# Cluster attention and two MoE layers on one core: the first pair's similarities from a dense centroid table, the last output tile in two halves, new order tables

## The chip, the cores and the metric

The kernel runs on one core of a Trainium2 chip. The metric is device time in microseconds (us) for one execution. A core has five engines that run side by side and wait for each other through semaphores: TensorE (PE; its weight loads are listed apart as PEld), VectorE (DVE), ScalarE (ACT), GpSimd (POOL) and SyncE (SP), which here only issues DMA transfers.

## The reference

Three stages, one after the other. `C` is 16 clusters, there are 2 batches of 8 heads with 768 positions of 64 values.

```python
q_n, k_n, c_n = (t / (norm(t) + 1e-6) for t in (q, k, centroids))
q_assign = argmax(einsum('bhsd,hcd->bhsc', q_n, c_n))
k_assign = argmax(einsum('bhsd,hcd->bhsc', k_n, c_n))
scores = where(q_assign[..., None] == k_assign[..., None, :], scale * q @ k.T, -1e9)
x = softmax(scores) @ v                      # then to [1536 tokens, 512]
h = x @ w_in; solu = h * softmax(h)
x = (layernorm(solu) * g_ln) @ w_out         # 512 -> 1024 -> 512
out = ((x @ w_a) * (x @ w_b)) @ w_out2       # 512 -> 1536 -> 512
```

## The kernel before

Heads are worked on in pairs: 8 pairs (batch, two heads), 96 score steps of 128 queries by 768 keys (`score`, L1014), each followed by the maximum (DVE L1018), the exponential (ACT L1022), transposes of the result (`turn`, L1046) and, for every three steps, the product with v (`apply`, L1070). Then come the first MoE layer (`moe_h` L1162, `moe_x2` L1254) and the second one (`quartet` L1384, `moe2_y` L1441), whose 12 output tiles are summed in PSUM, added to an accumulator in SBUF by DVE (L1457) and written out (SP L1460).

Every fp32 value that TensorE multiplies precisely is held as a high part and a low part ("hi" and "lo"). A head's operand `kq` has four slots of 768 columns; in slots 0 and 1 one half of the 128 rows holds the hi and the other half the lo part of q or k.

The mask is not applied to the scores one by one. Each query and key gets a one-hot row of its cluster, and these rows are a second matmul into the same PSUM tile. So before the first score of a pair can be complete, this must be done: transpose q and k (`direct`, PE L784, three transposes of 128 columns for each of q/k, head, half of the positions), take hi (ACT L791), a copy of hi into the other rows (ACT L796 for q, POOL L793 for k), take lo (DVE L797), multiply with the normalized centroids (`do_sim0`, PE L810), find the largest of the 16 (`do_arg`, DVE L879 to L890), transpose the one-hots (`do_oh0`, PE L905) and copy them into `kq` (ACT L916, DVE L914). This is the path of pair 0, and only of it: for the others `do_sims` (PE L841, L845) does it in other shapes, long ahead of need.

The centroids are normalized by seven small instructions (DVE L702 to L712, one POOL L704), doubled to 128 columns, transposed into PSUM (PE L717: rows 0 to 63 and 64 to 127 hold the same), and put into the table `cb`, which is mostly zeros: upper rows go to one set of columns and lower rows to another, hi (ACT L726) and lo (DVE L727). With this `cb`, one `do_sim0` matmul has 64 columns (hi and lo by row half by 16 clusters) and DVE has to add four of them up (L813).

To fill times in which TensorE has nothing to do at the start, `FILL` = 16 transposes of the identity (L719) and `WARM` = 8 matmuls of 512 columns (L732) stand in its queue; their results are not used.

The order of everything is written out: each engine's instructions are planned operations with a number, and the table `SEQ` lists for each engine the numbers in the order in which they are issued. Semaphores only make an engine wait; no engine ever passes a waiting instruction in its own list.

Of the kernel before, what the change touches and what calls it, by code (L numbers as in the profile page):

```python
# [49 lines left out]
        862, 829, 865, 853, 851, 873, 822, 866, 868, 887, 824, 876, 878, 900, 836, 890, 892, 903, 906, 904, 930,  # L50
        937, 935, 883, 947, 933, 944, 942, 910, 940, 954, 950, 948, 914, 973, 957, 959, 990, 979, 983, 961, 981,
        991, 997, 976, 993, 1004, 1015, 1006, 986, 1026, 1022, 1000, 1024, 1029, 1032, 1011, 1030, 1055, 1018,
        1041, 1044, 1046, 1020, 1074, 1058, 1036, 1069, 1060, 1038, 1075, 1081, 1077, 1051, 1084, 1096, 1086,
        1112, 1109, 1101, 1099, 1137, 1117, 1115, 1113, 1148, 1121, 1144, 1146, 1165, 1140, 1162, 1156, 1151,
        1154, 1176, 1168, 1166, 1158, 1190, 1181, 1172, 1204, 1179, 1201, 1199, 1186, 1197, 1216, 1211, 1193,
        1209, 1238, 1195, 1221, 1219, 1252, 1205, 1250, 1248, 1207, 1255, 1256, 1258, 1269, 1262, 1267, 1226,
        1287, 1265, 1282, 1285, 1280, 1278, 1310, 1290, 1288, 1292, 1317, 1313, 1315, 1327, 1320, 1322, 1324,
        1328, 1330, 1334, 1358, 1348, 1337, 1339, 1355, 1344, 1353, 1351, 1365, 1361, 1375, 1359, 1379, 1370,
        1368, 1386, 1384, 1382, 1389, 1392, 1390, 1403, 1396, 1399, 1401, 1413, 1408, 1406, 1410, 1416, 1414,
        1420, 1444, 1434, 1425, 1423, 1477, 1430, 1427, 1478, 1488, 1435, 1432, 1489, 1514, 1437, 1515, 1448,  # L60
        1454, 1547, 1544, 1541, 1548, 1580, 1577, 1581, 1613, 1574, 1610, 1614, 1646, 1607, 1643, 1647, 1670,
        1640, 1671, 1664, 1667, 1722, 1723, 1688, 1716, 1719, 1746, 1692, 1747, 1770, 1740, 1743, 1771, 1838,
        1689, 1693, 1696, 1700, 1697, 1701, 1764, 1839, 1793, 1832, 1767, 1788, 1794, 1789, 1835, 1803, 1798,
        1856, 1804, 1799, 1888, 1884, 1859, 1885, 1889, 1881, 1878, 1892, 1896, 1915, 1912, 1893, 1897, 1918,
        1922, 1923, 1919, 1930, 1926, 1931, 1927, 2053, 2055, 2057, 2059, 2061, 2064, 2066, 2068, 2070, 2072,
        2074, 2076, 2079, 2081, 2083, 2085, 2090, 2092, 2094, 2100, 2105, 2151, 2153, 2158, 2160, 2134, 2138,
        2133, 2137, 2135, 2168, 2162, 2201, 2173, 2205, 2203, 2209, 2207, 2141, 2136, 2143, 2147, 2149, 2139,
        2212, 2214, 2145, 2218, 2217, 2216, 2220, 2219, 2221, 2243, 2245, 2250, 2252, 2254, 2260, 2265, 2269,
        2229, 2231, 2230, 2273, 2271, 2277, 2275, 2312, 2232, 2234, 2233, 2309, 2307, 2282, 2280, 2308, 2310,
        2325, 2327, 2332, 2334, 2336, 2342, 2311, 2317, 2315, 2313, 2347, 2375, 2377, 2379, 2321, 2319, 2323,  # L70
        2391, 2381, 2383, 2386, 2388, 2418, 2420, 2425, 2390, 2392, 2394, 2395, 2427, 2429, 2435, 2440, 2409,
        2393, 2405, 2446, 2444, 2406, 2404, 2408, 2407, 2484, 2483, 2450, 2448, 2455, 2452, 2501, 2457, 2508,
        2503, 2487, 2512, 2510, 2485, 2486, 2491, 2489, 2488, 2518, 2523, 2551, 2553, 2555, 2557, 2559, 2562,
# [1463 lines left out]
```

## Time and profile before

| | |
|---|---|
| time, median of 3 runs | 681.65 us (680.88 to 681.95) |
| profiled execution | 681.25 us |
| its span in the trace | 679.4 us |
| PE / PEld busy | 671.3 us (99%) / 576.0 us (85%) |
| DVE / ACT / POOL busy | 523.1 / 389.4 / 285.8 us |
| chain that ended last | PE 93%, DVE 4%, ACT 1%, DMA 1%, issue 1% |

The span is the time from the first to the last event of the trace; the execution has 1.85 us around it. A busy share is the sum of the durations over the span. Matmuls overlap each other, so that a busy PE may still be one whose next matmul could have started earlier; how densely it works is seen from the starts of neighbouring instructions.

### The profile page before, as it was taken

The numbers are of one execution on the slowest core, as the hardware profiler recorded it, in microseconds if no ns is written. First come the engines' busy times: TensorE is split into PE (matmuls) and PEld (weight loads), VectorE is DVE, ScalarE is ACT, GpSimd is POOL, SyncE is SP. The second block draws the span as 40 slices with busy tenths as digits, with TensorE's granted clock in tenths as the row PEclk, the third lists the DMA queues.
The fourth block names the chain that finished last, engine by engine and source line by source line (L and its number), as shares of the span: only waits on it lengthen the run. The fifth ranks groups of instructions, "written<-read, shape, count | busy, mean of one in ns | idle before, by whom it ended". The sixth has DMA issues, their size and how long they took to land.

```text
span 679.4 us, 10935 instructions
## 1 busy us (share of the span) xinstructions
PE 671.3 (99%) x3910; PEld 576.0 (85%) x3910; DVE 523.1 (77%) x943; ACT 389.4 (57%) x820; POOL 285.8 (42%) x323
## 2 busy tenths in 40 slices
PE   8999999999999999999999999999999999999997
PEld 7777777777777767888999999998989999989996
DVE  6978797798778878999869359796876757977436
ACT  5877777768677864574464555554654543534221
POOL 4024554635456433244445477644335432542000
PEclk9999999999999999999999999999999999999999
DMA  4367447473722612110211002132112212110005
GB/s 140 97 157 192 115 119 189 121 169 83 203 85 71 161 38 63 32 62 32 66 59 62 1 1 91 65 116 72 62 63 94 93 63 63 63 62 32 1 0 187
DMA packets 33094, 58.49 MB, mean 86 GB/s; under 512 B 3848, under 2 KB 21904, under 8 KB 33040
## 3 DMA queue, kind: packets, MB, share of 16 engines
q1 hardware_dynamic: 33040, 57.79, 30.0%
q8 instruction: 31, 0.51, 0.3%
q14 instruction: 23, 0.19, 0.1%
HBM read 36.74 MB, written 3.15 MB: 59 GB/s over the span
## 4 chain that ended last, share of the span: by engine, by line
PE 93%; DVE 4%; ACT 1%; DMA 1%; issue 1%; SPq 0%; DVEq 0%; ACTq 0%
PE psT L1384 25%; PE psS L1162 10%; PE psO L1070 10%; PE psS L1441 9%; PE psS L1014 9%; PE psT L1046 9%; PE psO L1254 5%; PE psM L1254 5%; PE psO L1441 2%; PE psM L1441 2%; PE psT L1237 2%; PE psM L750 1%; PE psM L841 1%; PE psM L1099 1%; PE psM L845 1%; DMA R<-R 1%
## 5 line engine op out<-in xcount | busy, mean ns | idle before, releaser
L1384 PE MATMUL psT<-R 128*128 128x384 f32 x1008 | 181.8, 336 | 0.4 <-DVE F L1363 0.3
L1384 PEld LDWEIGHTS psT<-R 128*128 128x128 f32 x1008 | 175.8, 188 | 4.8 <-ACT F L1359 1.3
L483 POOL TENSOR_TENSOR R<-F,R 128x256 fp32r<-128x256 f32 (+3 forms) x92 | 109.7, 1202 | 98.0 <-ACT R L1294 51.5
L595 POOL TENSOR_TENSOR F<-F 128x512 int32<-128x512 int32 x45 | 60.8, 1350 | 110.3 <-DVE F L591 96.3
L1359 ACT COPY F<-psT 128x384 f32<-128x384 f32 x108 | 51.5, 480 | 91.9 <-PE psT L1384 84.8
L1022 ACT ACTIVATE F<-psS,mxn 128x768 f32<-128x768 f32 x96 | 86.7, 905 | 23.2 <-DVE mxn L1018 16.7
L1018 DVE TENSOR_REDUCE mxn<-psS 128x1 f32<-128x768 f32 x96 | 90.4, 951 | 10.6 <-PE psS L1014 9.4
L1014 PE MATMUL psS<-R 128*128 128x512 f32 (+3 forms) x384 | 89.9, 358 | 0.9 <-DMA R<-R 0.6
L1046 PE MATMUL psT<-ident,F 128*128 128x128 f32 x576 | 85.8, 275 | 0.2
L1046 PEld LDWEIGHTS psT<-ident,F 128*128 128x128 f32 x576 | 65.4, 140 | 13.3 <-ACT F L1022 6.3
L1014 PEld LDWEIGHTS psS<-R 128*128 128x128 f32 (+1 forms) x384 | 65.6, 190 | 12.2 <-ACT F L1022 2.6
L1441 PE MATMUL psS<-R 128*128 128x512 f32 x288 | 74.9, 391 | 0.0
L1162 PE MATMUL psS<-R 128*128 128x512 f32 x288 | 69.3, 394 | 0.0
L1070 PE MATMUL psO<-F 128*64 128x384 f32 x384 | 69.0, 494 | 0.0
L1053 DVE COPY F<-psT 128x384 f32<-128x384 f32 x96 | 52.8, 550 | 15.5 <-PE psT L1046 14.2
L1441 PEld LDWEIGHTS psS<-R 128*128 128x128 f32 x288 | 53.8, 188 | 10.3
L1162 PEld LDWEIGHTS psS<-R 128*128 128x128 f32 x288 | 53.0, 188 | 10.5
L485 DVE TENSOR_TENSOR R<-F,R 128x384 fp32r<-128x384 f32 (+1 forms) x72 | 53.3, 753 | 8.5 <-ACT R L1373 3.9
L1363 DVE TENSOR_TENSOR F<-psT,F 128x384 f32<-128x384 f32 x48 | 26.7, 555 | 39.8 <-PE psT L1384 35.0
L1055 ACT COPY F<-psT 128x384 f32<-128x384 f32 x96 | 45.9, 479 | 19.7 <-PE psT L1046 18.3
L1369 DVE TENSOR_TENSOR F<-F 128x384 f32<-128x384 f32 x60 | 44.3, 742 | 10.6 <-ACT F L1359 10.1
L1070 PEld LDWEIGHTS psO<-F 128*64 128x64 f32 x384 | 24.7, 136 | 28.2 <-issue 26.6
(158 smaller groups left out, 1000.2 us busy)
## 6 DMA issues: line engine op xcount, KB each, us to landing
F<-in_moe_w_out_dram SPq DMA_DIRECT2D x20, 512.0 KB, 3.3
R<-R SPq DMA_DIRECT2D x28, 288.0 KB, 4.4
F<-in_moe_w_a_dram SPq DMA_DIRECT2D x12, 512.0 KB, 3.7
F<-in_moe_w_b_dram SPq DMA_DIRECT2D x12, 512.0 KB, 3.6
R<-R SPq DMA_DIRECT2D x28, 192.0 KB, 3.9
F<-in_moe_w_in_dram SPq DMA_DIRECT2D x8, 512.0 KB, 4.9
F<-in_v_dram SPq DMA_DIRECT2D x8, 384.0 KB, 5.1
out_dram<-F SPq DMA_DIRECT2D x11, 256.0 KB, 2.6
```

The lines of the kernel that those rows point to most:

```text
L483: pl.add("POOL", pool(n), rank, lambda: G.tensor_tensor(out=out_, in0=in0, in1=in1, op=ALU.subtract), reads, writes)
L485: pl.add("DVE", dve(n), rank, lambda: V.tensor_tensor(out=out_, in0=in0, in1=in1, op=ALU.subtract), reads, writes, port=port)
L595: pl.add("POOL", pool(n), rank, lambda: G.tensor_tensor(out=ui, in0=ui, in1=low, op=ALU.add), [rk, lwk], [uk])
L1014: T.matmul(sp[:, c0:c0 + cn], kq[:r, 2 * m, t * P:(t + 1) * P], kq[:r, 2 * m + 1, c0:c0 + cn], start=m == 0, stop=m == 1)
L1018: pl.add("DVE", dve(S), i + SUB["max"], lambda: V.tensor_reduce(out=mxn[:, b:b + 1], in_=sp[:, :S], axis=AX.X, op=ALU.max, negate=True), [ ...
L1022: pl.add("ACT", act(S) + 93 + 93, i + SUB["exp"], lambda: A.activation(F[:, po:po + 768], sp[:, :S], AF.Exp, bias=mxn[:, b:b + 1], scale=1 ...
L1046: T.transpose(sp[:, c, :], pt[:, kt * P:(kt + 1) * P], ident)
L1070: T.matmul(psO[rs, :AN], vs[:, j, kt % HT * 2 + kt // HT], pt[:, kt, :], start=kt < 2, stop=kt >= NT - 2, tile_position=(0, kt % 2 * D), s ...
L1162: T.matmul(sp[:, n0:n0 + 512], xv5[:, i, a, c], winv[:, w, c, n0:n0 + 512], start=first, stop=(c == KD - 1 and a == 1))
L1254: T.matmul(sp[:, :GN], wo1v(f, w)[:, ds_], d[a][:, f, :], start=(f == 0 and x == 0), stop=(f == NF1 - 1 and x == 2))
L1384: T.matmul(t[:, :AN], wv[l][0][:, c], xp_[:, a, xi, c], start=(x in (0, 1, 3) and c == 0 and l == 0 and a == 0), stop=(c == 1 and l == 1), ...
L1441: T.matmul(yt, hy(j, a)[0][:, gg * P:(gg + 1) * P], R[:, wo + l * 512:wo + (l + 1) * 512], start=(u in first_u and fl == 0 and a == 0 and ...
```

## The change

Four edits.

1. The transposed centroids go as they are into a dense table of 128 rows: 128 columns of hi (one ACT copy) and 128 of lo (one DVE subtraction) in `R` at `CD_`. `do_sim0` multiplies with 16 columns of it, hi and lo after each other into the same PSUM columns, so that PSUM holds the finished similarity; the q and the k half of a head lie in one bank. The DVE additions (L813) are gone, and `do_arg` reads its first two inputs from PSUM.
2. `cb`, which the later pairs still need, is filled from the dense table by four ACT copies (`spread`). `WARM` reads the dense table.
3. The last output tile (`t == 0` of the last unit) leaves `moe2_y`. `last_y` computes it in two halves of 256 columns, each with all of its six matmuls, in the banks `psT1` and `psT0`, each half with its own addition and output DMA. The tile that was split before (`m == 2`) is not split any more.
4. All tables of `SEQ` are new.

```diff
@@ SEQ (all of its 186 lines; one of them)
-        18, 19, 20, 21, 22, 23, 24, 55, 25, 26, 51, 27, 43, 28, 29, 30, 17, 31, 47, 32, 33, 75, 110, 61, 59,
+        18, 19, 20, 21, 22, 23, 24, 53, 25, 26, 45, 27, 49, 28, 41, 29, 30, 31, 32, 17, 33, 108, 71, 75, 57, 79,
@@ centroids
-        cpv = psM[:, :P].rearrange("p (a h c) -> p a h c", a=NHP, h=2)
-        for r in range(2):
...
-            pl.add("ACT", act(128), Rk, lambda hi=hi, src=src: A.copy(hi, src), [mk, "cb0"], [("cb", 1 << r)])
-            pl.add("DVE", dve(128), Rk, lambda hi=hi, lo=lo, src=src: V.tensor_tensor(
-                out=lo, in0=src, in1=hi.bitcast(F32), op=ALU.subtract), [mk], [("cb", 1 << r)])
+        hi, lo = (R[:, CD_ + l * P:CD_ + (l + 1) * P] for l in range(2))
+        hk, lk = rc((CD_, P)), rc((CD_ + P, P))
+        pl.add("ACT", act(P), Rk, lambda: A.copy(hi, psM[:, :P]), ["psM"], [hk])
+        pl.add("DVE", dve(P), Rk, lambda: V.tensor_tensor(out=lo, in0=psM[:, :P], in1=hi.bitcast(F32), op=ALU.subtract), ["psM", hk], [lk])
+
+    def spread():
...
+                pl.add("ACT", act(P), Rk, lambda dst=dst, src=src: A.copy(dst, src.bitcast(F32)),
+                       [rc((CD_ + l * P, P), rows=1 << r), "cb0"], [("cb", 1 << r)])
@@ do_sim0
-        o = hp * 192 + f * 128
-        pv = bank[bk][:, :NT * 64].rearrange("p (t g c) -> p t g c", t=NT, g=4)
+        o = (2 * pairs[n][1] + f) * C
+        pv = bank[bk][:, :HT * 4 * C].rearrange("p (a s r c) -> p a s r c", a=HT, s=2, r=2)
 
         def mm():
             for t in range(NT):
-                T.matmul(pv[:, t], kq[:, s, t * P:(t + 1) * P], cb[:, o:o + 64], start=True, stop=True)
-
-        pl.add("PE", NT * 109, rk, mm, [rc((ko + s * 768, 768)), "cb"], [bk])
-        pl.add("DVE", dve(NT * 64), rk, lambda: V.tensor_reduce(
-            out=simv(n)[:, :, f, s].rearrange("p a r c -> p r a c"),
-            in_=pv.rearrange("p (r a) g c -> p r a c g", r=2), axis=AX.X, op=ALU.add), [bk], [simk(n, (s,), (f,))])
+                for l in range(2):
+                    c0 = CD_ + l * P + o
+                    T.matmul(pv[:, t % HT, s, t // HT], kq[:, s, t * P:(t + 1) * P], R[:, c0:c0 + C], start=l == 0, stop=l == 1)
@@ do_arg
-        pl.add("DVE", dve(n_), rk, lambda: V.reduce_max(out=m0, in_=oh, axis=AX.X), sk, [mk])
+        pl.add("DVE", dve(n_), rk, lambda: V.reduce_max(out=m0, in_=sim, axis=AX.X), [bk] if bk else sk, [mk])
         if on_dve:
-            pl.add("DVE", dve(n_), rk, lambda: V.tensor_tensor(out=oh, in0=oh, in1=bc(m0), op=ALU.is_equal), [mk], sk, port=True)
+            pl.add("DVE", dve(n_), rk, lambda: V.tensor_tensor(out=oh, in0=sim, in1=bc(m0), op=ALU.is_equal), [mk, bk] if bk else [mk], sk, port=not bk)
@@ last_y (new)
+            def mm(yt=yt, cs=cs):
+                for fl, j in fj:
+                    for a, l in ((0, 0), (0, 1), (1, 0)):
+                        c0 = w0[fl] + l * 512 + cs.start
+                        T.matmul(yt, hy(j, a)[0][:, :P], R[:, c0:c0 + DM // 2], start=(fl == 0 and a == 0 and l == 0), stop=(fl == 1 and a == 1))
```

The new tables move instructions on every engine. Three places are shown; names are the tiles, a trailing number after `x` counts instructions. First PE, from the centroids' transpose to the similarities of head 1 of pair 0 (L784: transposes of q and k; L810: `do_sim0`; L732: `WARM`), before:

```order
L717 MATMUL psM_70<-ident_71,F_64 128x128
L719 MATMUL psO_69<-ident_71 128x128
L784 MATMUL psT1_68<-ident_71,F_64 64x128 x3
L719 MATMUL psO_69<-ident_71 128x128 x2
L784 MATMUL psO_69<-ident_71,F_64 64x128 x3
L750 MATMUL psS1_66<-ident_71,F_64 128x128 x3
L810 MATMUL psT0_67<-cb_76,R_63 128x64 x6
L810 MATMUL psM_70<-cb_76,R_63 128x64 x6
L750 MATMUL psS1_66<-ident_71,F_64 128x128 x3
L784 MATMUL psO_69<-ident_71,F_64 64x128 x3
L784 MATMUL psT0_67<-ident_71,F_64 64x128 x3
L732 MATMUL psS1_66<-cb_76 128x512 x5
```

The same place of PE now, up to the last similarities of pair 0 (L792 is the old L784, L819 the old L810, L738 the old L732, L758 the old L750):

```order
L718 MATMUL psM_70<-ident_71,F_64 128x128
L720 MATMUL psO_69<-ident_71 128x128
L758 MATMUL psS1_66<-ident_71,F_64 128x128 x3
L792 MATMUL psO_69<-ident_71,F_64 64x128 x3
L792 MATMUL psT0_67<-ident_71,F_64 64x128 x3
L819 MATMUL psM_70<-R_63 128x16 x12
L792 MATMUL psO_69<-ident_71,F_64 64x128 x3
L792 MATMUL psT0_67<-ident_71,F_64 64x128 x3
L819 MATMUL psM_70<-R_63 128x16 x12
L758 MATMUL psS1_66<-ident_71,F_64 128x128 x3
L819 MATMUL psO_69<-R_63 128x16 x12
L738 MATMUL psS1_66<-R_63 128x512
```

Each group of six similarity matmuls became one of twelve; two transposes stand between the first two groups; of the five `WARM` matmuls that stood together only one is left here. Behind the piece shown come another twelve similarities, one and then three `WARM` (with the one-hot transposes between), four matmuls of `do_sims` (L847, before L841) that stood behind the first score, the first score, and the last three `WARM`, one of which stands directly ahead of the second score.

Second, ACT from its first copy to the centroid table (L791 and L796 are hi copies of q and k, L686 converts the identity, L726 fills `cb`), before:

```order
L791 ACTIVATE R_63<-psS1_66 64x384
L796 ACTIVATE R_63<-psS1_66 64x384
L791 ACTIVATE R_63<-psS0_65 64x384
L686 CAST F_64<-ident_71 128x128
L791 ACTIVATE R_63<-psT0_67 64x384
L796 ACTIVATE R_63<-psS0_65 64x384
L726 CAST cb_76<-psM_70 64x4x2x16 x2
```

The same place of ACT now (L799, L804, L687 are the old L791, L796, L686; L723 makes the dense hi table):

```order
L799 ACTIVATE R_63<-psS1_66 64x384
L799 ACTIVATE R_63<-psT1_68 64x384
L804 ACTIVATE R_63<-psS1_66 64x384
L799 ACTIVATE R_63<-psS0_65 64x384
L799 ACTIVATE R_63<-psT0_67 64x384
L804 ACTIVATE R_63<-psS0_65 64x384
L687 CAST F_64<-ident_71 128x128
L723 CAST R_63<-psM_70 128x128
```

A copy of k (from `psT1`) now stands second, and the centroid copy has six full copies and the identity ahead of it instead of five and the identity. On SP the first load of k was put ahead of the centroids' load.

Third, the end of PE (L1441: `moe2_y`), before:

```order
L1441 MATMUL psM_70<-R_63 128x512 x3
L1441 MATMUL psS0_65<-R_63 128x512 x3
L1441 MATMUL psO_69<-R_63 128x512 x6
L1441 MATMUL psS1_66<-R_63 128x512 x3
L1441 MATMUL psS0_65<-R_63 128x512 x3
```

The end of PE now (L1474 is the old L1441, L1453 the new `last_y`):

```order
L1474 MATMUL psO_69<-R_63 128x512 x3
L1474 MATMUL psS0_65<-R_63 128x512 x3
L1474 MATMUL psS1_66<-R_63 128x512 x3
L1453 MATMUL psT1_68<-R_63 128x256 x6
L1453 MATMUL psT0_67<-R_63 128x256 x6
```

The last thing to be computed, added and written was a tile of 512 columns and is now one of 256. Between these places, on PE from the second pair to the end, the groups keep nearly the same sequence; neighbours are exchanged.

## Rows read from the trace of the kernel before

**Rows 1.** The page: busy time by engine, then the granted TensorE clock in 40 slices.

```profile
PE 671.3 (99%) x3910; PEld 576.0 (85%) x3910; DVE 523.1 (77%) x943; ACT 389.4 (57%) x820; POOL 285.8 (42%) x323
...
PEclk9999999999999999999999999999999999999999
```

**Rows 2.** Windows: length, busy us of PE, PEld, DVE, ACT, POOL; clock, DMA.

```profile
15.00:20.00 5.00, 4.65 (x28) 3.96 (x28) 4.71 (x10) 3.26 (x8) 0.00 (x0) 1.00 0.49 176
...
25.00:30.00 5.00, 4.84 (x32) 2.77 (x31) 4.63 (x9) 3.86 (x9) 0.00 (x0) 1.00 0.88 217
...
100.00:200.00 100.00, 99.22 (x677) 73.80 (x673) 81.10 (x138) 75.88 (x165) 50.46 (x61) 1.00 0.60 148
200.00:300.00 100.00, 99.97 (x585) 76.64 (x585) 86.72 (x173) 64.08 (x125) 39.78 (x49) 1.00 0.25 67
...
400.00:500.00 100.00, 99.64 (x525) 92.30 (x524) 81.07 (x127) 55.41 (x116) 54.83 (x45) 1.00 0.24 80
```

**Rows 3.** Timeline of the start: start us, duration us, engine, line, operation.

```profile
3.23 0.85 PE L784 MATMUL psS<-ident,F 128*64 128x128 f32 x3
...
5.18 0.48 ACT L791 ACTIVATE R<-psS 64x384 fp32r<-64x384 f32 x1
...
5.57 0.28 ACT L686 CAST F<-ident 128x128 bf16<-128x128 f32 x1
...
6.08 0.49 PE L784 MATMUL psT<-ident,F 128*64 128x128 f32 x3
...
6.41 0.38 PE L719 MATMUL psO<-ident 128*128 128x128 f32 x2
...
6.77 0.53 ACT L726 CAST cb<-psM 64x128 fp32r<-64x128 f32 x2
...
7.40 0.59 DVE L727 TENSOR_TENSOR cb<-psM,cb 64x128 fp32r<-64x128 f32 x2
...
8.13 0.83 PE L810 MATMUL psT<-cb,R 128*128 128x64 f32 x6 [0.69 <-ACT R L791]
...
8.79 0.83 PE L810 MATMUL psM<-cb,R 128*128 128x64 f32 x6
...
9.67 0.56 DVE L813 TENSOR_REDUCE F<-psM 128x96 f32<-128x384 f32 x1
...
10.26 0.35 DVE L879 TENSOR_REDUCE mx<-F 128x12 f32<-128x192 f32 x1
...
11.50 0.55 DVE L797 SCALAR_TENSOR_TENSOR R<-psT,R 64x384 fp32r<-64x384 f32 x1
...
13.55 0.89 DVE L890 TENSOR_SCALAR F<-F 128x96 bf16<-128x96 bf16 x1
```

**Rows 4.** Timeline of the first scores, same columns; one row of DVE's second L890.

```profile
15.93 0.96 PE L1014 MATMUL psS<-R 128*128 128x512 f32 x4
...
16.73 0.87 PE L841 MATMUL psM<-R,cb 128*128 128x384 f32 x4
...
17.43 0.87 PE L1014 MATMUL psS<-R 128*128 128x512 f32 x4
...
21.82 0.18 DVE L890 TENSOR_SCALAR F<-F 128x96 bf16<-128x96 bf16 x1
```

**Rows 5.** Timeline of the end, same columns.

```profile
672.50 1.52 PE L1441 MATMUL psO<-R 128*128 128x512 f32 x6
...
673.86 1.52 PE L1441 MATMUL psS<-R 128*128 128x512 f32 x6
674.06 0.76 DVE L1457 TENSOR_TENSOR F<-psO,F 128x256 f32<-128x256 f32 x2 [0.67 <-PE psO L1441]
674.74 1.37 DVE L1457 TENSOR_TENSOR F<-psS,F 128x512 f32<-128x512 f32 x2
```

**Rows 6.** Output DMAs of the end: count, KB each, median us to landing.

```profile
out_dram<-F SPq DMA_DIRECT2D x11, 256.0 KB, 2.6
out_dram<-F SPq DMA_DIRECT2D x2, 128.0 KB, 1.8
```

More of the change, by code (lines that the diff above doesn't have):

```diff
@@ L801, in do_sim0 @@
     def do_sim0(n, s, f, rk, bk):
[L803 removed]
         kq, ko = kqv(2 * n + f), kqo(2 * n + f)
[L805 to L806 removed]
+        o = (2 * pairs[n][1] + f) * C
+        pv = bank[bk][:, :HT * 4 * C].rearrange("p (a s r c) -> p a s r c", a=HT, s=2, r=2)
         def mm():
             for t in range(NT):
[L810 to L815 removed]
+                for l in range(2):
+                    c0 = CD_ + l * P + o
+                    T.matmul(pv[:, t % HT, s, t // HT], kq[:, s, t * P:(t + 1) * P], R[:, c0:c0 + C], start=l == 0, stop=l == 1)
+        pl.add("PE", 2 * NT * 109, rk, mm, [rc((ko + s * 768, 768), (CD_, 2 * P))], [bk])
     def do_place(n, j, part, rk):
@@ L1122, in tile_cluster_attention_moe_moe2 @@
     task(-140, centroids)
+    task(-40, spread)
     task(-39, warm)
@@ L1428, in tile_cluster_attention_moe_moe2, with last_y @@
     left = {us[-1]: sum(1 for b2, v in visits[i + 1:] if b2 == b) for i, (b, us) in enumerate(visits)}
+    def last_y(u, b):
+        o = ACC_[b * NT]
+        rk = T1 + (u + 2) * U
+        fj = [(fl, j) for j, (fl, half_) in enumerate(YO) if half_ == 0]
+        hk = [rc((HY_ + j * 2 * AN, P), (HY_ + (j * 2 + 1) * AN, P)) for fl, j in fj]
+        w0 = [WY_[(u // 2 * 2 + fl) % 3] for fl in range(2)]
+        for x in range(2):
+            yt, yk, cs = psT[x][:, :DM // 2], f"psT{x}", slice(x * DM // 2, (x + 1) * DM // 2)
+            av, fk = F[:, o + cs.start:o + cs.stop], fc((o + cs.start, DM // 2))
+            def mm(yt=yt, cs=cs):
[3 more added lines that the diff above has]
+                        T.matmul(yt, hy(j, a)[0][:, :P], R[:, c0:c0 + DM // 2], start=(fl == 0 and a == 0 and l == 0), stop=(fl == 1 and a == 1))
+            pl.add("PE", mm_cost(DM // 2, 6), rk + x * 0.6, mm, [*hk, *[rc((w, 1024)) for w in w0]], [yk])
+            pl.add("DVE", dve(DM // 2), rk + x * 0.6 + 0.1, lambda av=av, yt=yt: V.tensor_tensor(out=av, in0=yt, in1=av, op=ALU.add), [yk], [fk])
+            dma(128, rk + x * 0.6, lambda av=av, cs=cs: Y.dma_start(outv[b, 0, 0, :, cs], av), [fk], [])
     def moe2_y(u, j):
@@ L1436, in moe2_y @@
             yt, yk = yv[t]
+            if u == NU - 1 and t == 0:
+                if fl:
+                    last_y(u, b)
+                continue
             rk = T1 + (u + (1.5 if u == 0 else 1) + (j * 3 + gg + 0.5) / (28 if u == 0 else 14)) * U
@@ L1452, in moe2_y @@
             else:
-                m = 2 if u == NU - 1 and j == 3 and gg == 2 else 1
-                for x in range(m):
-                    cs = slice(x * DM // m, (x + 1) * DM // m)
-                    fk = fc((o + cs.start, DM // m))
-                    pl.add("DVE", dve(512 // m), rk + 0.1, lambda av=av[:, cs], yt=yt[:, cs]: V.tensor_tensor(
-                        out=av, in0=yt, in1=av, op=ALU.add), [yk], [fk])
-                    if not left[u]:
-                        dma(256 // m, rk, lambda av=av[:, cs], t=t, cs=cs: Y.dma_start(outv[b, t // HT, t % HT, :, cs], av), [fk], [])
+                fk = fc((o, 512))
+                pl.add("DVE", dve(512), rk + 0.1, lambda av=av, yt=yt: V.tensor_tensor(out=av, in0=yt, in1=av, op=ALU.add), [yk], [fk])
+                if not left[u]:
+                    dma(256, rk, lambda av=av, t=t: Y.dma_start(outv[b, t // HT, t % HT], av), [fk], [])
     pl.add("NOP", 0, -1e9, lambda: None, [], [part("sim"), part("ohp"), fc((SIM_, OHP_ + 768 - SIM_))])
```

24 lines of the change are left out of this document (14 added, 10 removed), and 336 rows, old and new, of the table SEQ.

## The prediction

> **What bounds the kernel now.** The page comes first: PE is busy 671.3 of 679.4 us, every other engine much less, and the granted clock is full in all slices [rows 1]. So a change can gain only where PE idles, or where it does work that need not be done. The windows say where it idles [rows 2]: 0.35 us between 15 and 20, 0.16 between 25 and 30, and in the long middle 0.78, 0.03 and 0.36 us in the three stretches that are not full. That is 1.7 us of waiting in the 660 us behind the first score. The rest lies ahead of the first score, at 15.93 us, and behind the last matmul. The timeline of the start [rows 3] shows why the first score is so late: one chain runs through all engines, from the centroid table (ready when DVE L727 ends, 7.99 us) over the similarities (8.13 and 8.79), their addition on DVE (L813), the largest of 16 (L879, from 10.26) to the one-hots (L890, ended 14.44). The timeline of the end [rows 5] shows the other place: the last six matmuls start at 673.86 and end at 675.38, DVE's last addition ends at 676.11, and then the output DMA and the end of the program take 3.3 us.
>
> My sum is made against the profiled execution of 681.25 us, 1.85 us more than its span; the median of the runs is 0.40 us above it. A change below 0.2% (1.36 us) can't be told from none by a measurement of this kernel.
>
> **What one similarity matmul costs.** Six with 64 columns start at 8.13 and the next six at 8.79 [rows 3], 0.110 us each. Three transposes of 128 columns and what follows them (6.08 to 6.41) also take 0.110 each, while 512 columns take 0.227 (six from 672.50 to 673.86 [rows 5]). From 128 columns down the moving columns no longer show. Every matmul has its own weight load: 3910 of each [rows 1]. The kernel has pairs of matmuls with the same stationary tile behind each other already (hi and lo in L1162 and L1441), and they save no load. So 12 matmuls of 16 columns should cost 12 x 0.110 = 1.32 us against 0.66, if nothing about 16 columns is cheaper. There is no row for 16 columns; the bounds are 0.66 (a pair costs what one did) and 1.32 us a group, and I take 1.32, the price of the nearest rows. The Trainium skill, page "TensorE: Matmul & The Clock Gate", gives in its section "Back-to-back issue gap" about 25 ns as the gap between matmuls of up to 64 columns; by it a group of twelve would take 0.3 us and the four groups 4.1 us less than I reckon. The row of 0.110 us for 64 columns disagrees with it, and agrees with the section "LDWEIGHTS (loading the stationary operand)" of the same page, by which a load goes by its 128 columns, some 107 ns, whatever is multiplied.
>
> **The start, step by step.** The four similarity groups of pair 0 cost 48 x 0.110 instead of 24 x 0.110: +2.64 us of PE work ahead of the first score. What makes room for it?
>
> The table. Its two ACT copies (0.53) become one (0.28, as the identity's L686), its two DVE subtractions (0.59) one of about 0.3. But ACT now has six hi copies and the identity ahead of it. The second of these is a copy of k, which takes the place of the copy at 5.18; from there five copies of 0.49, the identity's 0.28 and the copy's 0.28 end at 8.2, DVE's subtraction at 8.5, and the K similarities start near 8.6, 0.45 later than 8.13. The centroids' load, now behind k's, may land up to a microsecond later: DVE's seven small instructions end at 5.67 (start of the last: 5.38), and ACT is free for the result only at 7.9, so this is hidden; it costs something only beyond some 1.5 us.
>
> The path. K similarities 8.6 to 9.9, two groups of transposes (0.33 each), Q similarities to 11.9. Before, the two groups and DVE's additions were over at 10.23. So the first maximum starts at about 12.0 instead of 10.26. From there to the one-hots it was 4.2 us (10.26 to 14.44). Of this, one L797 (0.55) stands no longer in between, and L890 took 0.89 where its second run took 0.18 [rows 4]; part of that may return. That makes 3.0 to 3.6 and the one-hots end at 15.0 to 15.6, 0.6 to 1.2 us later than before.
>
> PE meanwhile is not idle: the similarities of head 1 (2.64), transposes and two of the `WARM` matmuls fill it to about 15.5. One-hot transposes, three `WARM` (0.235 each) and four matmuls of `do_sims` (0.70, 16.73 to 17.43 [rows 4]) follow, and the first score starts near 17.3. Now compare equal work: before, the first score and this `do_sims` were done at 17.43; now at 17.3 + 0.8 = 18.1, so 0.65 us later. Three `WARM` that before were over still stand ahead of the second and third score: +0.70 if PE has something better to do there. Against it stands what DVE no longer has to do: four additions of 0.56 and the second head's assignment, which now is mostly done ahead of the first score. DVE is busy 4.71 and 4.63 of 5 us around there [rows 2]; if that is what PE waited for, the 0.35 + 0.16 us of idle go. So the start is 1.35 us later at worst, 0.15 later if the three `WARM` fall into waits and no other wait shrinks, 0.4 earlier if both happen. I take +0.6, the middle of what is likely. If the price of a similarity is the lower bound, 2 x 0.66 come off the path and the start is 0.7 us earlier.
>
> `spread` is four ACT copies (4 x 0.27) ahead of `do_sims`, in a stretch where ACT is busy 3.26 of 5 us [rows 2]: hidden by that idle time; 1.1 us if it were not.
>
> **The end.** Six matmuls of 512 columns become twelve of 256. 256 lies between the 64 columns at 0.110 and what a score allows: its two of 512 and two of 256 take 0.80 (15.93 to 16.73), which less 2 x 0.227 leaves at most 0.173 each. So 1.32 to 2.08 us against 1.36; I take 1.5, nearer to the row of weight loads, so +0.14. DVE's last addition has 256 columns: 0.38 (two in 0.76) instead of 0.69, -0.31 [rows 5]. The last DMA has 128 KB: 1.8 us to landing against 2.6 [rows 6], but these are medians of a full queue; between 0 and -0.8 I take -0.4. Sum -0.57, from -1.0 to +0.4. The tile that was split before and is not any more has two others behind it, which hide it.
>
> **The middle.** PE's groups keep their sequence but for neighbours. No instruction is added there. What new neighbours wait for, the order doesn't tell; all that is to be had is the 1.17 us of idle behind 100 us [rows 2], and I allow as much for new waits. I take 0.
>
> Sum: +0.6 - 0.57 + 0 = 0.0, so 681.3 us for an execution like the profiled one, 681.7 beside the median.
>
> **Rivals.**
>
> *The additions on DVE were the bound, and dense similarities are cheap* (chance 0.28). For it: DVE is over 92% busy from 15 to 30 us; the chain loses two L813. Against it: the price of weight loads. At 0.66 a group the start is 0.7 us earlier, the end 0.57, and with the idle of the middle gone too, 1.2: 679.2 to 680.4, middle 679.7.
>
> *The clock falls* (chance 0.13; ends slower). The granted clock was full because PE was kept working: at 3.23 three transposes took 0.85 us, at 6.08 only 0.49 [rows 3], and it stayed full from then on. Between 8 and 12 us five matmuls of 512 columns and twelve of 64 ran; now it is 24 of 16 columns and six transposes, and the `WARM` come later. If the clock does not stay up with that and goes to 1.2 GHz for some us, PE's work behind it, which is on the path there (similarities of head 1, `do_sims`: 3.3 us), takes up to twice as long: +1.7 to +3.3, 683.4 to 685. Against it: PE is busy with weight loads all the time. It decides from the moment a slice of the start shows a clock below 1.00.
>
> *The tables of the middle bring a new wait* (chance 0.09): one place like the longest idle stretch now, with a price of 0.8 to 1.7 us, mostly behind a transfer on SP, whose list is new throughout: 682.5 to 683.4.
>
> **Chances.** My forecast, PE-paced start and a shorter end, has 0.50 and its own range is 680.5 to 682.9. It is faster by over 0.2% (below 680.3) in 0.04, slower (above 683.0) in 0.04. The first rival is faster in 0.25 of its 0.28, the second slower in 0.11 of 0.13, the third slower in 0.03 of 0.09. Faster 0.29, slower 0.18, same 0.53. The range takes in the first rival and the near end of the second: 679.4 to 683.5.
>
> **What would show it.** L819 groups of twelve start 1.3 us apart: the price. L723 starts near 7.9 and the first L819 near 8.6: ACT's list. The first maximum (L886) near 12 and the first score near 17.3. The last L1453 group takes 1.5 us, the addition behind it 0.38. The five-us windows of the middle still idle some 1.2 us. I am wrong if twelve similarities take 0.7 us, if the clock of a window at the start is below 1.00, or if the windows behind 100 us idle by over 2 us.

## The result and the profile after

The changed kernel takes 685.38 us (median of 6 executions, 684.21 to 686.47), the kernel before 681.38 us beside it: ratio 1.0058, 95% interval 1.0047 to 1.0068. It is 4.0 us slower; I had forecast 681.7 us and most likely no measurable change.

The page of the changed kernel: PE's total, and the granted clock in 40 slices.

```profile
PE 676.6 (99%) x3940; PEld 582.0 (85%) x3940; DVE 519.1 (76%) x938; ACT 390.0 (57%) x823; POOL 286.7 (42%) x323
...
PEclk9899999999999999999999999999999999999999
```

Against [rows 1], DVE has 4.0 us less to do and PE 5.3 us more. The added similarities, 24 at 0.11 us, are only half of that, and the second slice shows an 8 where there were only nines. The windows say where (length, busy us of PE, PEld, DVE, ACT, POOL; clock; DMA):

```profile
10.00:15.00 5.00, 5.00 (x41) 4.91 (x41) 3.26 (x8) 3.51 (x9) 2.74 (x5) 0.87 0.49 161
15.00:20.00 5.00, 5.00 (x20) 3.91 (x20) 3.10 (x8) 1.40 (x3) 1.88 (x3) 0.50 0.36 98
20.00:25.00 5.00, 5.00 (x30) 4.32 (x30) 3.17 (x6) 2.50 (x5) 0.55 (x2) 0.94 0.00 0
25.00:30.00 5.00, 4.79 (x37) 3.91 (x36) 4.49 (x8) 4.36 (x11) 0.97 (x1) 1.00 0.74 226
...
100.00:200.00 100.00, 99.56 (x679) 74.03 (x678) 81.76 (x141) 75.94 (x167) 50.40 (x64) 1.00 0.60 145
200.00:300.00 100.00, 100.00 (x595) 76.84 (x594) 85.69 (x170) 65.08 (x131) 44.03 (x52) 1.00 0.29 78
...
400.00:500.00 100.00, 99.66 (x533) 93.51 (x532) 83.45 (x126) 56.67 (x118) 56.16 (x47) 1.00 0.23 70
```

A clock of 0.87, 0.50 and 0.94 means that 1.3, 5.0 and 0.6 us of these windows were granted at half (1.2 GHz): 6.9 us together. PE idles nowhere in these three, and DVE, 4.71 of 5 us busy from 15 to 20 before [rows 2], now has 3.10: the engine that the start waits for has become PE. The middle is as predicted, 0.44 + 0 + 0.34 us of idle against 0.78 + 0.03 + 0.36.

The timeline of the start of the changed kernel (start us, us, engine, line, operation): PE's similarities (L819), DVE's first maximum (L886) and the end of the first one-hots (L897), `do_sims` (L847) and the first score (L1021):

```profile
8.71 1.51 PE L819 MATMUL psM<-R 128*128 128x16 f32 x12
...
10.67 1.49 PE L819 MATMUL psM<-R 128*128 128x16 f32 x12
12.01 0.55 PE L758 MATMUL psS<-ident,F 128*128 128x128 f32 x3
12.19 0.36 DVE L886 TENSOR_REDUCE mx<-psM 128x12 f32<-128x192 f32 x1
...
12.31 1.48 PE L819 MATMUL psO<-R 128*128 128x16 f32 x12
...
14.15 2.57 PE L819 MATMUL psO<-R 128*128 128x16 f32 x12
...
15.55 0.37 DVE L897 TENSOR_SCALAR F<-F 128x96 bf16<-128x96 bf16 x1
...
19.74 1.25 PE L847 MATMUL psM<-R,cb 128*128 128x384 f32 x4
20.82 0.86 PE L1021 MATMUL psS<-R 128*128 128x512 f32 x4
```

The first three groups follow the forecast: twelve from 10.67 to 12.01 are 0.112 each, the first maximum starts at 12.19, the one-hots end at 15.92 (forecast 15.0 to 15.6). The fourth group takes 2.57 instead of 1.48 us: here the clock has fallen. The first score starts at 20.82 instead of 15.93.

The timeline of its end answers to [rows 5]:

```profile
677.66 1.59 PE L1453 MATMUL psT<-R 128*128 128x256 f32 x12
678.57 0.42 DVE L1456 TENSOR_TENSOR F<-psT,F 128x256 f32<-128x256 f32 x1
...
679.29 0.42 DVE L1456 TENSOR_TENSOR F<-psT,F 128x256 f32<-128x256 f32 x1 [0.29 <-PE psT L1453]
```

And its output DMAs of the end to [rows 6]:

```profile
out_dram<-F SPq DMA_DIRECT2D x11, 256.0 KB, 2.1
out_dram<-F SPq DMA_DIRECT2D x2, 128.0 KB, 1.9
```

From the start of the last group to the end of the span there are now 682.4 - 677.66 = 4.74 us, before 679.4 - 673.86 = 5.54: 0.8 us less. The last group itself starts 3.8 us later (677.66 for 673.86), so the start lost 3.8 us in this execution. It is the fastest of the six, 1.2 us below the median.

### The profile page after: what moved, and what is told of

It reads as the page before. It is cut to its first block, busy times and chain, and to the rows that moved or that the text cites. A ratio compares the mean times of both kernels' runs of the same rounds, so it can differ in the third digit from the quotient of the medians.

```text
span 682.4 us, 10997 instructions
## 1 busy us (share of the span) xinstructions
PE 676.6 (99%) x3940; PEld 582.0 (85%) x3940; DVE 519.1 (76%) x938; ACT 390.0 (57%) x823; POOL 286.7 (42%) x323
## 4 chain that ended last, share of the span: by engine, by line
PE 96%; DMA 1%; DVE 1%; ACT 1%; SPq 0%; issue 0%; ACTq 0%; DVEq 0%
PE psT L1392 25%; PE psS L1021 10%; PE psS L1170 10%; PE psO L1077 9%; PE psS L1474 9%; PE psT L1053 9%; PE psM L1262 5%; PE psO L1262 5%; PE psM L1474 2%; PE psO L1474 2%; PE psT L1245 2%; PE psM L847 1%; PE psM L758 1%; PE psM L1106 1%; PE psM L851 1%; DMA R<-R 1%
## 5 line engine op out<-in xcount | busy, mean ns | idle before, releaser
L596 POOL TENSOR_TENSOR F<-F 128x512 int32<-128x512 int32 x45 | 62.7, 1395 | 104.2 <-DVE F L592 95.8
L1021 PE MATMUL psS<-R 128*128 128x512 f32 (+3 forms) x384 | 89.6, 358 | 0.4 <-DMA R<-R 0.4
L1021 PEld LDWEIGHTS psS<-R 128*128 128x128 f32 (+1 forms) x384 | 65.5, 190 | 10.6 <-ACT F L1029 1.1
L1474 PE MATMUL psS<-R 128*128 128x512 f32 x282 | 72.7, 391 | 0.0
L1170 PE MATMUL psS<-R 128*128 128x512 f32 x288 | 69.3, 394 | 0.0
L1474 PEld LDWEIGHTS psS<-R 128*128 128x128 f32 x282 | 52.7, 188 | 10.0
L1294 DVE TENSOR_TENSOR F<-F 128x256 f32<-128x256 f32 x72 | 39.3, 565 | 17.4 <-ACT F L1274 8.4
```

The source lines that it names most:

```text
L596: pl.add("POOL", pool(n), rank, lambda: G.tensor_tensor(out=ui, in0=ui, in1=low, op=ALU.add), [rk, lwk], [uk])
L1021: T.matmul(sp[:, c0:c0 + cn], kq[:r, 2 * m, t * P:(t + 1) * P], kq[:r, 2 * m + 1, c0:c0 + cn], start=m == 0, stop=m == 1)
L1170: T.matmul(sp[:, n0:n0 + 512], xv5[:, i, a, c], winv[:, w, c, n0:n0 + 512], start=first, stop=(c == KD - 1 and a == 1))
L1474: T.matmul(yt, hy(j, a)[0][:, gg * P:(gg + 1) * P], R[:, wo + l * 512:wo + (l + 1) * 512], start=(u in first_u and fl == 0 and a == 0 and ...
```

## The experiments

The theory after this reading: the clock fell because the 16-column similarities and the later `WARM` left PE busy, but with narrow work (matmuls of few columns, each behind a weight load). Rival 1: the dense similarities and what waits for them cost 4 us at full clock too. Rival 2: only the place of the `WARM` counts. Each execution has a mean granted clock: the kernel before has 0.996 to 1.000 in all, the changed one 0.993 in five of six and 0.995 in the profiled one. The mean also counts the last microseconds, where the clock falls in every trace behind the last matmul (that of before has 0.88 from 670 us on), so a difference of 0.002 says nothing about the start.

**Three edits apart.** In the changed kernel, the `WARM` among the similarities (they use `psS0` instead of `psS1`; W stands for one `WARM`, sK, sQ for head 0's similarities, s1 for head 1's, oh for one-hot transposes):

```diff
-    PE: sK, sQ, s1, W, s1, oh, W, oh, W W W, do_sims, score, W W, ..., W, score
+    PE: sK, sQ, W W W W W, s1, W, s1, oh, W, oh, W, do_sims, score, ..., score
```

> The changed kernel with its eight WARM matmuls of 512 columns spread among the 16-column similarities (five behind the Q group of head 0, three more between the groups of head 1) instead of five of them standing right ahead of the first score; everything else as changed. Theory (the clock fell because nothing but narrow matmuls ran from 8.7 to 13.7 us, and that is the loss): the granted clock is 1.00 in all windows of the start, first score at 17.2 to 18.5 us, time 681.0 to 682.6 us. Rival 1 (the dense similarities and the later assignment cost 4 us by themselves): clock 1.00 too, but the first score stays behind 19.5 us and the time at 684.5 or more. Rival 2 (only the place of the WARM matmuls counts): as the theory.

Measured: 683.85 us (ratio 1.0036, 1.0024 to 1.0048), mean clock 0.995 to 0.997. In the trace the clock is 1.00 until 15 us, then 0.85 and 0.81 in the next two windows: 1.5 + 1.9 = 3.4 us at half instead of 6.9. More wide work early put the fall off and halved it. No expectation is met: the theory had wanted a full clock, and the time lies between it and rival 1.

The kernel before, with only its `WARM` moved back:

```diff
-    PE: sK, sQ, ..., W W W W W, s1, oh, W, oh, W W, s1, score, do_sims, score
+    PE: sK, sQ, ..., s1, W, oh, W, oh, W W W, s1, score, W W, do_sims, W, score
```

> The kernel before, its 64-column similarities kept, with the WARM matmuls moved back to where the changed kernel has them (two among the similarities of head 1, three ahead of the similarities of the kind L845, three behind the first score). Theory (the narrow similarities are needed for the fall): the clock stays at 1.00, time within 0.7 us of the kernel before. Rival 2 (the place of the WARM matmuls alone does it): the clock falls in the windows 10 to 20 us, time 683 to 685.5. Rival 1: no change from before beyond 0.7 us.

Measured: 683.62 us, but in two heaps. Four of eight executions had a clock of 0.998 to 1.000 and took 681.47 to 682.55 us, the other four had 0.992 to 0.995 and took 684.70 to 686.81. So the place of the `WARM` alone can make the clock fall, without one of the 16-column similarities, but doesn't in each execution. The traced one kept its clock, so the place of the fall is not seen. Between the heaps' medians lie 3.3 us. And with the clock full the late `WARM` still cost 1.0 us (682.27, the median of these four, against 681.27).

Only the last tile in two halves, everything else as before (`last_y` of the diff above, added to the kernel before):

> The kernel before, with only the last tile in two halves of 256 columns (the function last_y), in the order of before. Prediction's term for the end: -0.57 us; trace of the changed kernel (last matmul to the end of the span 3.15 us instead of 4.04): -0.9. So 680.5 to 680.9 us. A rival, that the two halves' DMAs land no earlier together than the one before: 681.2 to 681.8.

Measured: 681.20 us beside 681.27 (ratio 0.9997, 0.9988 to 1.0005), as the rival has it: no gain that can be told from none. The trace shows that the end's gain is smaller here than in the changed kernel. Its last group in the timeline:

```profile
673.19 1.59 PE L1458 MATMUL psT<-R 128*128 128x256 f32 x12
```

Its output DMAs of the end:

```profile
out_dram<-F SPq DMA_DIRECT2D x11, 256.0 KB, 3.1
out_dram<-F SPq DMA_DIRECT2D x2, 128.0 KB, 2.2
```

From the last group to the end of the span (678.5) there are 5.31 us, 0.2 less than before; the small DMA lands in 2.2 us behind others that take 3.1. In the changed order these take 2.1, and the end gains 0.8. All eight traces with the new order have 4.69 to 4.76 us there, the five with the whole tile 5.54 to 5.58. That the earlier DMAs make the difference between 0.2 and 0.8 is not shown.

**More columns at the same price.** The changed kernel with 40 columns in each similarity, 24 of which nothing reads:

```diff
-        pv = bank[bk][:, :HT * 4 * C].rearrange("p (a s r c) -> p a s r c", a=HT, s=2, r=2)
+        pv = bank[bk][:, :HT * 4 * 40].rearrange("p (a s r c) -> p a s r c", a=HT, s=2, r=2)
...
-                    T.matmul(pv[:, t % HT, s, t // HT], kq[:, s, t * P:(t + 1) * P], R[:, c0:c0 + C], start=l == 0, stop=l == 1)
+                    T.matmul(pv[:, t % HT, s, t // HT], kq[:, s, t * P:(t + 1) * P], R[:, c0:c0 + 40], start=l == 0, stop=l == 1)
```

> The changed kernel, in its own order, with similarities of 40 columns instead of 16 (the other 24 columns are computed and not read). A similarity costs the same 0.110 us at full clock by its weight load. Theory in its narrow form (too few moving columns while PE waits for nothing): more columns for the same time, so the clock falls later, for a shorter time or not at all; 681.5 to 684.5 us. If the columns don't count, and only the kind of work around does: the clock record and the time stay as with the changed kernel, 685 to 686 us.

Measured: 684.21 us (683.17 to 684.76), clock 0.993 to 0.997. It is 1.2 us less than the changed kernel, measured at another time (ratios to before 1.0041 and 1.0058), but in the trace the half-clock stretch is as long as there (0.90, 0.50 and 0.91: 6.9 us). Alone it settles nothing.

Both edits together, 40 columns and the early `WARM`:

> The two edits of the runs before together: 40-column similarities (24 columns computed and not read) and the eight WARM matmuls among them. PE's time per instruction is as in e1_warm_early. Theory (the clock falls where narrow matmuls make up most of a stretch; neither edit alone was enough, with the clock half for 3.4 and 6.8 us): the clock stays full through 10 to 25 us, first score at 18 to 19 us, time 681.0 to 682.3, the start costing about the 0.6 us of the prediction. Rival 1 (the dense similarities cost some 3 us at full clock too): clock full, but 683 to 685. If columns do not count: as e1_warm_early, half for some 3.4 us, 683.4 to 684.2.

Measured: 683.27 us (ratio 1.0033, 1.0021 to 1.0045); in the profiled execution (682.99) the clock is full from beginning to end, in the others 0.995 to 0.997. Its windows from 15 to 30 us:

```profile
15.00:20.00 5.00, 5.00 (x34) 4.00 (x33) 3.18 (x8) 1.88 (x4) 2.32 (x3) 1.00 0.37 98
20.00:25.00 5.00, 4.67 (x33) 3.75 (x32) 4.41 (x8) 4.12 (x9) 1.51 (x2) 1.00 0.21 47
25.00:30.00 5.00, 4.18 (x29) 3.25 (x27) 4.58 (x8) 3.64 (x8) 0.00 (x0) 1.00 1.04 275
```

Its timeline at the first score, and at the first product with v:

```profile
18.45 0.86 PE L1033 MATMUL psS<-R 128*128 128x512 f32 x4
...
30.63 2.16 PE L1089 MATMUL psO<-F 128*64 128x384 f32 x12 [1.23 <-DMA F<-in_v_dram]
```

This is the changed kernel's work at full clock, with the `WARM` earlier, and it is 1.7 us above the profiled execution of before (681.25): the last group starts 2.6 us later than before (676.47), and the shorter end gives 0.8 back. The first score starts 2.4 us earlier than at the fallen clock, and PE has new idle time behind it, most of it one wait of 1.23 us for v. The chain of waits ends in a load of v that was issued at 23.87 and took 6.62 us to land:

```profile
23.87 6.62 DMA F<-in_v_dram
```

By this wait the lead of 2.4 us shrinks to 1.1 at the first product with v (31.72 in the changed kernel), and the two executions end 1.2 us apart. By the medians (685.38 and 683.27) it is 2.1. So by these two kernels the clock is 1.2 to 2.1 us of the 4, and rival 1 holds for the rest.

Fourteen `WARM` instead of eight, 16 columns:

> The changed kernel with 16-column similarities, and with fourteen WARM matmuls instead of eight, spread among and behind them up to the first score; six more cost 6 x 0.227 = 1.4 us of PE, all ahead of the first score. Theory: the clock stays full from the first rise on; first score at 19 to 20 us, time 682.2 to 683.6, so faster than the changed kernel (685.4) although it does more. Rival 1 (the loss is work on the path, not the clock): the added work adds to it, 685.5 to 687. If narrow matmuls make the clock fall however much wide work stands between them: 684 to 687 with a half-clock stretch.

Measured: 685.63 us (683.47 to 688.67). One execution of six kept a clock of 1.000 and took 683.47; the profiled one (685.09) has clocks of 0.87 and 0.79 from 15 to 25 us, 3.4 us at half. Six more wide matmuls did not hold the clock safely, and the median is above that of eight early ones (683.85). The third expectation is the one that came true; the range of rival 1 holds the median too, but it has no fall of the clock in it.

**The clock alone.** The kernel before without its `WARM`:

```diff
-WARM = 6000.0, 8
+WARM = 6000.0, 0
```

> The kernel before without its eight WARM matmuls, which compute nothing that is read. 8 x 0.227 = 1.8 us less work on PE, and nothing else changed: no dense similarities, no new order. Theory (clock): the clock falls to half in the windows between 10 and 22 us in most executions, the time is 684 to 687. Rival 1 (clock of no weight): 680 to 681.5.

Measured: 683.10 us beside 681.04 (ratio 1.0030, 1.0020 to 1.0040), clock 0.992 to 0.997. Nothing was added, 1.8 us of PE work that nobody reads was taken out, and the kernel is 2.1 us slower, less than the 684 to 687 expected. Its windows from 10 to 25 us:

```profile
10.00:15.00 5.00, 3.10 (x24) 2.20 (x22) 4.69 (x10) 2.68 (x6) 3.29 (x5) 0.87 0.23 64
15.00:20.00 5.00, 4.98 (x19) 4.48 (x18) 3.66 (x8) 1.92 (x6) 0.11 (x1) 0.50 0.55 196
20.00:25.00 5.00, 5.00 (x36) 4.11 (x35) 4.27 (x9) 4.24 (x11) 1.36 (x2) 0.95 0.00 0
```

Its timeline, the first score and `do_sims` behind it:

```profile
16.57 1.63 PE L1026 MATMUL psS<-R 128*128 128x512 f32 x4
17.99 1.48 PE L853 MATMUL psM<-R,cb 128*128 128x384 f32 x4
```

The same three windows, 6.8 us at half (1.3 + 5.0 + 0.5) as against 6.9 in the changed kernel; the score takes 1.63 us instead of 0.96 [rows 4]. But here PE idled 1.90 of the 5 us from 10 to 15, 1.44 of them in one wait for DVE just ahead of the fall, so this is not the fall of a busy engine. PE works off 3.4 us less, and 2.1 us reach the end, the 1.8 us taken out and the new idle time included. The length of the fall hardly shows in the time: two executions with a mean clock of 0.997 took 682.96 and 683.00 us, the six with 0.992 to 0.994 took 682.93 to 683.90.

**The work at full clock.** The kernel of the two edits together, with the product with the low part of the centroids left out (half of the similarities):

```diff
-                for l in range(2):
+                for l in range(1):
```

> e6_sims40_warm_early with the product with the low part of the centroid table left out: 24 similarity matmuls instead of 48 for the first pair, so 24 x 0.110 = 2.6 us less on PE, 1.3 us of it ahead of the first maximum; all else as there (683.3 us, first score at 18.45 us with the clock full). If PE's time for the doubled similarities sets the start at full clock: first score at 16.0 to 17.0 us, time 680.6 to 681.8. If another engine or a transfer sets it: first score moves by less than 1 us, 682.4 to 683.3.

Measured: 681.94 us (681.19 to 683.12), clock 0.997 to 1.000; ratio to before 1.0011 (1.0002 to 1.0020). So 1.3 us less than with all similarities; executions with a mean clock of 1.000 alone differ by 1.1 (medians 681.87 of six here, 682.99 of three in the kernel with all similarities and the one in the next paragraph). The time lies between the two expectations. The first score is at 17.68, 0.8 us earlier, and rows of its timeline say why it isn't earlier still:

```profile
4.75 0.22 DVE L715 SCALAR_TENSOR_TENSOR F<-F 128x64 f32<-128x64 f32 x1 [4.75 <-DMA F<-in_centroids_dram]
...
8.93 0.85 PE L831 MATMUL psM<-R 128*128 128x40 f32 x6
...
17.05 0.79 PE L859 MATMUL psM<-R,cb 128*128 128x384 f32 x3 [0.52 <-POOL R L780]
```

The same two places in the trace with all similarities:

```profile
4.22 0.23 DVE L715 SCALAR_TENSOR_TENSOR F<-F 128x64 f32<-128x64 f32 x1 [4.22 <-DMA F<-in_centroids_dram]
...
8.40 1.52 PE L831 MATMUL psM<-R 128*128 128x40 f32 x12
```

The centroids landed 0.53 us later in this execution, and the first similarities started 0.53 us later. At 17.05 PE waits 0.52 us for POOL's subtraction for pair 1. So of the 2.6 us taken off PE about half reach the end.

This kernel has as many similarities as the one before, and is still 0.7 us slower. Where does that go? Three of its windows, with the idle time of PE:

```profile
5.00:10.00 5.00, 4.13 (x31) 3.15 (x30) 4.01 (x13) 4.09 (x10) 1.71 (x4) 1.00 0.26 96
...
15.00:20.00 5.00, 4.10 (x20) 2.84 (x20) 4.43 (x11) 2.30 (x5) 1.92 (x3) 1.00 0.38 102
...
100.00:200.00 100.00, 98.76 (x675) 73.44 (x674) 80.13 (x139) 75.07 (x165) 50.48 (x64) 1.00 0.59 142
```

The first of them before ([rows 2] has the others):

```profile
5.00:10.00 5.00, 4.32 (x38) 4.07 (x37) 4.64 (x12) 3.29 (x10) 1.46 (x3) 1.00 0.21 79
```

From 5 to 30 us PE idles 2.13 us in this trace against 1.48 before, from 100 to 200 us 1.24 against 0.78. The trace is 0.5 us longer than that of before: 1.1 us more of waits, less the 0.8 that the shorter end gives back, and a few tenths that are not located.

**The centroids' load,** second on SP's queue again (first in the kernel of the two edits, then in the changed one):

```diff
-    SP: q, k, centroids, k, k, q, ...
+    SP: q, centroids, k, k, k, q, ...
```

> e6_sims40_warm_early with the load of the centroids issued second on SP's queue again, as before the change, instead of third behind k's first load. DVE's first instruction, which waits for it, began at 3.34 to 3.43 us in four traces of kernels with the load second and at 3.84 to 5.54 us in five with it third; ACT is ready for the table's copy near 7.6 to 8.1 us, which corresponds to a landing near 4.4. If the late landing is part of the loss: DVE begins at 3.3 to 3.5 us, K similarities near 8.3 in each execution, time 682.2 to 683.0 and less spread. If it is hidden as I predicted: 683.1 to 683.5.

> The changed kernel with that one issue put back, and nothing else. The clock falls as in the changed kernel. If the late landing is part of the loss: 684.4 to 685.1 us. If it is hidden: 685.2 to 685.6.

Measured: 683.15 us (682.56 to 684.28) beside the earlier 683.27, and 685.03 (684.70 to 685.98) beside 685.38. DVE's first instruction did start at 3.30 and 3.44 us again, but the differences of 0.1 and 0.35 us are smaller than the spread. The first lies in the range for a hidden load and the second in that for a late one; against before, the ratios hardly move (1.0033 to 1.0028, and 1.0058 to 1.0059). So no price of the late load can be told from none. Hidden it was not: in five of the six traces with the load third the first similarities start 4.17 or 4.18 us behind DVE's first instruction, at 8.40 to 9.71; only in the changed kernel's own (3.84 and 8.71) is there slack. With the load second they started at 8.85 and 9.90, no earlier. The chain of the trace with two edits goes from the centroids' load through DVE: its subtractions of lo (L817, the old L797) stand behind the centroids' instructions in its list, and the transposes ahead of the similarities wait for them.

**The dense similarities in the old order.** The kernel before with the edits on the table, the similarities and the assignment alone; its order, its `WARM` and its end unchanged:

```diff
-    PE: s (6 of 64 columns), s (6), ..., W W W W W, s (6), ...
+    PE: s (12 of 16 columns), s (12), ..., W W W W W, s (12), ...
```

> The kernel before with the dense table, the doubled 16-column similarities summed in PSUM and the assignment in place, but with the order of before: centroids' load second, WARM matmuls where they were, K similarities ahead of Q's, the last tile whole. DVE's four additions of 0.56 us and the two table copies fall away, PE has 24 similarity matmuls more (2.6 us). If the new order is what loses the time (clock through the place of the WARM, and the rest): 680.8 to 682.0 us, clock 1.00. If the doubled similarities cost 1.3 us wherever they stand, as e9_hi_only against e6_sims40_warm_early suggests: 682.2 to 682.9 with the clock full. If 16 columns make the clock fall even with five WARM right behind the first groups: 683 to 685 and a stretch at half.

Measured: 686.06 us (684.43 to 686.65; ratio 1.0072, 1.0058 to 1.0085), clock 0.992 in three of five, 0.994 and 0.998 in the others (685.26 and 684.43 us). The stretch at half is as the third expectation has it, the time is above its range. This is the clearest one. Its timeline, the first two groups and the five `WARM`:

```profile
7.55 2.85 PE L831 MATMUL psM<-R 128*128 128x16 f32 x24 [0.23 <-DVE R L736]
...
11.37 2.49 PE L750 MATMUL psS<-R 128*128 128x512 f32 x5
```

Its windows from 10 to 25 us:

```profile
10.00:15.00 5.00, 5.00 (x26) 4.09 (x25) 3.18 (x8) 2.18 (x5) 2.77 (x4) 0.66 0.08 20
15.00:20.00 5.00, 5.00 (x32) 4.37 (x32) 1.46 (x3) 3.20 (x10) 0.81 (x2) 0.82 0.79 234
20.00:25.00 5.00, 5.00 (x18) 4.50 (x18) 3.22 (x6) 2.02 (x4) 0.00 (x0) 0.50 0.02 6
```

The two groups stand together (24 from 7.55 to 10.25, 0.112 each), and right behind them the five `WARM` take 2.49 us instead of the 1.43 of the next kernel below: the wide work comes too late, it already runs at the half clock. The clock comes back and falls again in the second half of the windows, 3.4 + 1.8 + 5.0 = 10.2 us in all. So the new order is not needed for the fall.

The same kernel with 40 columns:

> e3_dense_old_order with similarities of 40 columns instead of 16 (24 columns computed and not read), so the same instructions, waits and PE time at full clock, but more moving columns. In that trace the clock was half in 11.4 to 14.8 and 18.3 to 25.1 us and the time 686.1. If the columns of the similarities are what lets the clock fall: less or no time at half, 682 to 684.5 us. If only the number of short matmuls matters: the same half-clock stretches, 685.5 to 686.6.

Measured: 685.48 us, in two heaps again: three executions at a clock of 0.994 with 685.48 to 685.88, two at 1.000 with 683.41 and 683.80. Its matmuls cost the same, 24 from 8.15 to 10.83, as its timeline shows:

```profile
8.15 2.83 PE L831 MATMUL psM<-R 128*128 128x40 f32 x24
...
11.96 1.43 PE L750 MATMUL psS<-R 128*128 128x512 f32 x5
```

Its windows from 15 to 25 us:

```profile
15.00:20.00 5.00, 5.00 (x29) 4.25 (x29) 1.31 (x3) 2.53 (x8) 1.41 (x2) 0.75 0.67 236
20.00:25.00 5.00, 5.00 (x22) 4.59 (x22) 3.47 (x7) 2.37 (x5) 0.00 (x0) 0.57 0.00 0
```

Here the `WARM` run at full clock, the first fall is gone and the second is there (2.5 + 4.3 us). With more columns the fall is shorter in the trace and missing in two of five executions (with 16 columns in one at most, that of 0.998), but not gone: each expectation holds for one heap. Between the heaps lie 2.0 us, the price of the fall once more.

## Why the prediction was wrong

**Of the 4.0 us, some 2 are the clock, by an estimate.** No execution of the changed kernel kept its clock, so the price comes from its neighbours: 2.1 us (the kernel before without its `WARM`), 2.0 (the two heaps of the last kernel), 3.3 (the two heaps of the kernel before with late `WARM`), and 2.1 by the medians or 1.2 by the traces (the changed kernel against the one with two edits, whose `WARM` also stand earlier). The step that failed is in the rival: "Against it: PE is busy with weight loads all the time." PE was busy 5.00 of 5 us and the clock fell nonetheless. The place was right (the similarities of head 1 took up to 1.7 times as long, 2.57 us for 1.48) and so was the mark by which to know it; the chance of 0.13 was not. I had read from [rows 3] that the clock rises on transposes of 128 columns, and taken any work for good enough. Two causes are shown, each by itself: the dense similarities with the `WARM` where they were (a mean clock of 0.994 or less in four of five executions), and late `WARM` with the similarities of before (in four of eight). How far the first is the number of the similarities and how far their 16 columns stays open.

**The rest is the start at full clock.** My term was +0.6, with -0.57 of the end against it. In the trace at full clock the start costs 2.6 us. The two executions at full clock of the old-order kernel with 40 columns, without the shorter end, stand 2.4 and 2.8 above that comparison's 680.99. The price of a similarity (0.112 measured for 0.110) and the start of the first maximum (12.19 for 12.0) were right. The step that failed is the overlap: I let the added work of PE fall into its waits, and let "the 0.35 + 0.16 us of idle go". At full clock PE idles 0.33 + 0.82 us from 15 to 30 us and 0.63 in the five us behind, most of it in the wait for v. A wait behind a transfer on SP, which my third rival had put into the middle, is there at the start. Half of the similarities cost 1.1 to 1.3 us: that part is shown. DVE lost four additions, 2.2 us, but the chain went over to PE, which got 2.6 us more, and DVE then waited: 3.18 of 5 us busy from 15 to 20 in the trace at full clock, against 4.71 [rows 2]; its longest wait there, 1.49 us, is for PE's similarities. The late `WARM` (+0.70 if not hidden) cost 1.0 in the kernel before, at full clock. My sum was off as well: +0.65 and +0.70 with 0.51 of idle to be had give +0.14 to +1.35, not down to -0.4.

**The end** was forecast at -0.57: the traces show -0.8 in the new order and -0.2 with the old one. PE's group took 0.07 us more than before (1.59 for 1.52; predicted +0.14), the addition 0.42 (0.38). The rest of the gain is not explained here, and in the times of whole executions the end alone can't be told from nothing.

**The middle** was forecast at 0, and it is: PE's idle time in the three stretches behind 100 us was 1.17 us and is 0.78. **The first rival,** DVE as the bound and cheap similarities, fell by both of its parts. `spread` was hidden, as costed: no wait of PE in the traces names it. The centroids' load was not: I had looked at ACT, which would take its result late anyway, and overlooked what stands behind it in DVE's list.

No kernel here beats the one before. The only piece of the change that was shown not to lose is the divided last tile, and it doesn't win measurably.

## What to carry to other kernels

TensorE at 100% busy can lose its clock: in these kernels it fell to half with PE busy 5.00 of 5 us, behind a stretch of short matmuls. So before wide matmuls are replaced by narrow ones, or work that computes nothing is moved or taken out, look at what it was good for: find the stretch of the granted clock, and reckon with a fall there as a likely case, priced by a kernel in which only that filler is left out. And an addition taken from one engine gains nothing when the chain then runs through the engine that got the work.

## What the runs showed that I had not expected

A kernel can stand at the edge: with the same instructions in the same order, four of eight executions kept the clock and four lost it, 681.5 to 682.6 against 684.7 to 686.8 us. Six more `WARM` matmuls made the spread wider (683.5 to 688.7), not narrower. And twelve matmuls of 16 columns take as long as twelve of 40 (0.112 us each, with its own weight load for each, though two in a row use the same stationary tile): the first group of the changed kernel takes 1.36 us (8.71 to 10.07).

The Trainium skill, page "TensorE: Matmul & The Clock Gate", section "Back-to-back issue gap", states about 25 ns as the gap for up to 64 columns, for matmuls without their weight loads; by it that group would take some 0.3 us, an estimate. The same section says that in a stream of loads and matmuls both set the spacing, so the 0.110 us of the prediction did not disagree with it: the figure was for another case. No run here has such matmuls without loads.
